# Keys in three tiles of 128 plus one shared rest tile, with the instruction order planned in passes

## The chip, the cores and the metric

The kernel runs on one core of one Trainium2 chip. The metric is device microseconds of that core for one execution. Runs of 3 to 5 rounds give an interval; executions of one kernel agree within about 0.3 to 0.5 %. "Faster" or "slower" needs more than 2 %. In the profiles PE is TensorE (the matmuls), ACT is ScalarE (exponentials, roots), DVE is VectorE and POOL is GpSimd (squares, sums, scalings), SP is SyncE (it issues transfers), and DMA stands for the transfers themselves.

## The reference

```python
def rmsnorm(x, g):
    return x / np.sqrt(np.mean(x * x, axis=-1, keepdims=True) + 1e-06) * g
q_n, k_n = rmsnorm(q, g_q), rmsnorm(k, g_k)         # q, k, v: 8 batches, 12 heads, 448 tokens, 64 dims, float32
scores = np.matmul(q_n, k_n.transpose(0, 1, 3, 2)) / 8
attn = softmax(scores)                              # written out in the reference
x = np.matmul(attn, v)                              # -> 3584 tokens x 768
h = x @ w_in                                        # 768 x 2048
out = (h * np.clip(h + 3.0, 0.0, 6.0) / 6.0) @ w_out    # 2048 x 768
```

A batch has six pairs of heads, so there are 48 pairs. The order of the keys does not matter as long as the values use the same order; both kernels use this freedom.

## The kernel before

Every instruction is a step given to a planner. The planner is a list scheduler: it walks forward in time, and on each engine it takes, of the steps that could start, the one with the smallest hand-set `due` time. The result is a fixed order per engine. On the chip each engine then runs its own list strictly in order and waits by semaphores.

```python
    NPE = 10
    GATE, W_IN_AT, W_OUT_AT, W_STEP = 2, 7.0, 35.0, 6.3
    START, FIRST, PAIR = 9.0, 4.1, 2.3
...
    def load_g():                                   # four small loads on ScalarE's queue
        for a in range(2):
            nc.scalar.dma_start(out=gq_t[a * 64:(a + 1) * 64, :], in_=g_q.rearrange("(p o) -> p o", o=1))
            nc.scalar.dma_start(out=gk_t[a * 64:(a + 1) * 64, :], in_=g_k.rearrange("(p o) -> p o", o=1))
...
    def heads(src, P):                              # keys: 4 tiles of 112; 1024 contiguous bytes per partition and head
        b, j = divmod(P, NJ)
        return src[b, 2 * j:2 * j + 2, :, :].rearrange("h (p t) d -> p h (t d)", t=T)
...
            def score(t0=t0, taken=taken):          # a cluster: four 64-row matmuls, two heads side by side
                for i, (ps, _, _) in enumerate(taken):
                    for a in range(2):
                        rows, c0 = slice(a * 64, a * 64 + 64), (t0 + i) * PT
                        nc.tensor.matmul(out=ps[:, a, 0:S], lhsT=kp[rows, c0:c0 + 128],
                                         rhs=kq[rows, 1, :], start=True, stop=True)
...
        def values(dst, c0, first):                 # 2 heads x 4 key tiles, for each of 4 query tiles: 32 matmuls
            for a in range(2):
                for t in range(T):
                    nc.tensor.matmul(
                        out=dst[:, a * E1:(a + 1) * E1], lhsT=e[0:PT, t, a, c0:c0 + 128], rhs=va[0:PT, a, t, :],
                        start=(first and a == 0 and t == 0), stop=(t == T - 1), skip_group_check=True)
...
    def weights(c, at, load, kept):                 # w_in and w_out, four loads of 768 KB each, on GpSimd's queue
        kept[c] = add("POOL", 0.9, at, lambda: load(c), gate, xfer=4.4, after=at)
```

The MLP of batch b is interleaved with the attention of batch b + 1. Batch 0's attention therefore runs alone. I call the time up to about 140 us the ramp; after that everything repeats every 50 us or so.

## Time and profile before

| stretch | PE busy | what runs |
|---|---|---|
| 0 to 11.7 us | 0.0 | loads, squares, root |
| 11.7 to 45.5 us | 26.2 of 33.8 | batch 0's attention alone |
| 45.5 to 80 us | 32.3 of 34.5 | first MLP, batch 1's attention |
| 80 to 376 us | 293.9 of 296 | steady state |
| 376 to 434 us | 57.9 of 58 | last MLP |

The median time is 441.08 us. The page of the kernel before, its parts 1 and 2: the busy time of TensorE, then 40 slices of 11 us each with the busy tenths of TensorE, the granted clock, the busy tenths of the DMA engines, and what they moved.

```profile
PE 410.6 (94%) x3663; PEld 229.2 (52%) x3682; DVE 246.3 (56%) x417; ACT 249.0 (57%) x425; POOL 240.2 (55%) x230
PE   0588799999999999999999999999999999999995
PEclk9999999999999999999999999999999999999999
DMA  8999999877545745674465655684465420220122
GB/s 241 247 265 261 224 214 193 216 197 192 128 121 148 189 113 136 167 214 111 133 156 157 177 135 145 159 214 109 120 161 164 97 56 12 54 81 0 37 72 73
```

TensorE is full from the sixth slice on. The DMA engines are full (tenths 8 and 9) from the first slice to the seventh, about 77 us.

The view by stretches of the same kernel (stretch, its length, busy us and instructions of PE, PEld, DVE, ACT, POOL, granted clock, DMA share, GB/s; the DMA share adds up the times of packets, which overlap, so it can exceed 1):

```profile
20.00:40.00 20.00, 18.30 (x250) 11.86 (x250) 17.98 (x36) 17.32 (x27) 17.83 (x18) 1.00 1.16 260
40.00:60.00 20.00, 15.79 (x186) 9.65 (x188) 17.52 (x30) 13.09 (x27) 19.45 (x22) 1.00 1.22 228
60.00:80.00 20.00, 19.84 (x207) 11.33 (x208) 14.55 (x27) 16.44 (x29) 16.86 (x16) 1.00 1.08 209
80.00:120.00 40.00, 39.46 (x353) 20.24 (x358) 27.10 (x39) 26.98 (x45) 27.46 (x24) 1.00 0.69 177
```

The timeline of GpSimd, reduced to the weight loads that it issues (start, length; the first, the last w_in, and the last w_out); each lands about 10 to 13 us later, the last at 69.3 us:

```profile
8.34 1.04 POOL L277 DMA_DIRECT2D w_in_sb<-in_moe_w_in_dram  x1
...
34.31 0.89 POOL L277 DMA_DIRECT2D w_in_sb<-in_moe_w_in_dram  x1
...
57.06 0.94 POOL L283 DMA_DIRECT2D w_out_sb<-in_moe_w_out_dram  x1
```

In the waits of 0 to 14 us (us in total, times, longest), ScalarE's first square waits 6.9 us behind its own g loads:

```profile
ACT sq L320 <- DMA gq_t<-in_g_q_dram: 6.9, 1, 6.9
```

In the groups by form (line, engine, operation, shapes, count, then busy us in total and mean ns of one), there are 192 exponentials, and VectorE's five squares of the ramp average 1354 ns:

```profile
L421 ACT ACTIVATE e<-S 112x896 bf16<-112x896 f32 x192 | 166.3, 914 | 64.1 <-PE S L416 64.0
...
L322 DVE TENSOR_TENSOR sq<-qk 112x512 f32<-112x512 f32 x5 | 6.8, 1354 | 0.0
```

### The profile page before, as it was taken

How to read it: one execution, taken by the hardware profiler on the slowest of the kernel's cores; microseconds unless marked ns; L12 is line 12 of the kernel's file. 1: busy time of each engine (PE TensorE's matmuls, PEld its weight loads, DVE VectorE, ACT ScalarE, POOL GpSimd, SP SyncE). 2: the span in 40 equal slices, each digit the busy share in tenths (PEclk: the TensorE clock that was granted, in tenths of full speed). 3: DMA queues.
4: the chain of work that ended last, by engine and by line, in shares of the span. 5: the costliest groups of instructions: out<-in, count | busy, mean ns of one | idle time of the engine just before them, and what ended most of it. 6: DMA issues, size and time to landing. Idle time of an engine off the chain costs nothing.

```text
span 438.6 us, 9205 instructions
## 1 busy us (share of the span) xinstructions
PE 410.6 (94%) x3663; PEld 229.2 (52%) x3682; DVE 246.3 (56%) x417; ACT 249.0 (57%) x425; POOL 240.2 (55%) x230
## 2 busy tenths in 40 slices
PE   0588799999999999999999999999999999999995
PEld 0355455555455565554455565554455555654563
DVE  1998887657674564456555465556564444334421
ACT  3788588657765666367664677357673665123200
POOL 3499988855757567656765657747757510000000
PEclk9999999999999999999999999999999999999999
DMA  8999999877545745674465655684465420220122
GB/s 241 247 265 261 224 214 193 216 197 192 128 121 148 189 113 136 167 214 111 133 156 157 177 135 145 159 214 109 120 161 164 97 56 12 54 81 0 37 72 73
DMA packets 102923, 64.58 MB, mean 147 GB/s; under 512 B 59744, under 2 KB 99424, under 8 KB 102880
## 3 DMA queue, kind: packets, MB, share of 16 engines
q1 hardware_dynamic: 94544, 57.01, 50.6%
q0 software_dynamic: 7296, 6.29, 9.1%
q10 hardware_dynamic: 1040, 0.69, 0.5%
q8 instruction: 29, 0.48, 0.5%
q14 instruction: 14, 0.11, 0.1%
HBM read 45.61 MB, written 11.01 MB: 129 GB/s over the span
## 4 chain that ended last, share of the span: by engine, by line
PE 80%; POOL 5%; DVE 4%; ACT 3%; issue 3%; DMA 3%; SPq 1%; POOLq 0%
PE M L558 27%; PE M L533 25%; PE S L416 9%; PE X L437 8%; PE S L558 4%; PE R L437 2%; PE S L533 2%; DVE ssq L337 1%; ACT e L421 1%; POOL qks L351 1%; PE X L558 1%; POOL sq L322 1%; POOL va L359 1%; DMA gq_t<-in_g_q_dram 1%; POOL sq L329 1%
## 5 line engine op out<-in xcount | busy, mean ns | idle before, releaser
L421 ACT ACTIVATE e<-S 112x896 bf16<-112x896 f32 x192 | 166.3, 914 | 64.1 <-PE S L416 64.0
L533 PE MATMUL M<-xT,w_in_sb 128*128 128x384 bf16 (+1 forms) x679 | 145.1, 349 | 3.7 <-DVE gT L541 2.9
L351 POOL TENSOR_TENSOR qks<-qk,rs 112x512 bf16<-112x512 f32 x87 | 90.5, 1055 | 86.6 <-ACT rs L344 84.7
L558 PE MATMUL M<-w_out_sb,gT 128*128 128x384 bf16 x736 | 131.8, 326 | 0.0
L558 PEld LDWEIGHTS <-gT 128*128 128x128 bf16 x896 | 82.9, 98 | 57.8 <-issue 7.8
L533 PEld LDWEIGHTS <-w_in_sb 128*128 128x128 bf16 x768 | 69.6, 97 | 67.4 <-issue 12.5
L541 DVE SCALAR_TENSOR_TENSOR gT<-t,M 128x384 bf16<-128x384 f32 (+1 forms) x116 | 70.6, 611 | 59.1 <-ACT t L539 58.3
L539 ACT ACTIVATE t<-M 128x384 f32<-128x384 f32 (+1 forms) x116 | 62.6, 540 | 67.0 <-PE M L533 65.5
L437 PEld LDWEIGHTS <-e 112*128 112x128 bf16 x1536 | 65.1, 99 | 31.4 <-issue 16.0
L337 DVE TENSOR_REDUCE ssq<-sq 112x16 f32<-112x1024 f32 (+1 forms) x49 | 58.4, 1193 | 23.3 <-POOL sq L329 12.2
L329 POOL TENSOR_TENSOR sq<-qk 112x1024 f32<-112x1024 f32 x36 | 68.1, 1892 | 0.0
L416 PE MATMUL S<-kq,kp 64*128 64x448 bf16 x384 | 56.6, 364 | 4.1 <-DVE kp L381 1.7
L437 PE MATMUL X<-va,e 112*128 112x65 bf16 x1152 | 58.6, 196 | 0.8 <-ACT e L421 0.6
L566 DVE COPY y<-M 128x384 f32<-128x384 f32 x46 | 25.6, 556 | 59.2 <-PE M L558 59.0
L359 POOL CAST va<-vf 112x512 bf16<-112x512 f32 x48 | 31.5, 658 | 10.4 <-DMA vf<-in_v_dram 10.1
L392 POOL TENSOR_SCALAR kp<-kq,gp 128x448 bf16<-128x448 bf16 x23 | 32.3, 1402 | 5.3 <-DMA kq<-qks 5.2
L463 DVE TENSOR_TENSOR xn<-X,rd 128x384 bf16<-128x384 f32 x48 | 26.8, 558 | 1.6
L416 PEld LDWEIGHTS <-kp 64*128 64x128 bf16 x384 | 12.2, 94 | 27.7 <-issue 18.0
L437 PE MATMUL R<-va,e 112*128 112x65 bf16 x384 | 20.4, 195 | 0.0
L377 PE MATMUL M<-ident,qks 112*128 112x112 bf16 x80 | 7.9, 242 | 13.0 <-DVE qks L351 12.4
L558 PE MATMUL S<-w_out_sb,gT 128*128 128x384 bf16 x112 | 19.5, 326 | 0.0
L462 DVE RECIPROCAL rd<-X 128x6 f32<-128x6 f32 x48 | 9.2, 192 | 15.3 <-PE X L437 15.2
(42 smaller groups left out, 156.2 us busy)
## 6 DMA issues: line engine op xcount, KB each, us to landing
qk<-in_k_dram SPq DMA_DIRECT2D x48, 224.0 KB, 3.3
vf<-in_v_dram SPq DMA_DIRECT2D x48, 224.0 KB, 3.7
qk<-in_q_dram SPq DMA_DIRECT2D x45, 224.0 KB, 3.4
w_in_sb<-in_moe_w_in_dram POOLq DMA_DIRECT2D x4, 768.0 KB, 11.3
w_out_sb<-in_moe_w_out_dram POOLq DMA_DIRECT2D x4, 768.0 KB, 11.9
out_dram<-y SPq DMA_DIRECT2D x8, 336.0 KB, 3.1
out_dram<-y SPq DMA_DIRECT2D x8, 288.0 KB, 3.4
out_dram<-y SPq DMA_DIRECT2D x8, 240.0 KB, 3.2
```

What stands on the lines that cost most here:

```text
L329: parts = [add("POOL", 1.93, at - 10, lambda: nc.gpsimd.tensor_tensor(out=sq[0:PT], in0=qk[0:PT], in1=qk[0:PT], op=MULT), *ld, *war, lock= ...
L337: red = add("DVE", 0.6 * n, at - 8 * hurry + 0.5 * i0, lambda i0=i0, i1=i1, cs=cs: nc.vector.tensor_reduce(out=ssq[0:PT, cs], in_=sq[0:PT, ...
L351: sc.append(add(on, 0, at - 6 * hurry, lambda e, i=i, rs4=rs4: engines[e].tensor_tensor(out=qks[0:PT, i].rearrange("p t h d -> p h t d"), ...
L359: vc = add({"POOL": 0.61}, 0, at - 3, lambda e: engines[e].tensor_copy(out=va[0:PT, :, :, 0:D], in_=vf[0:PT].rearrange("p h (t d) -> p h t ...
L392: nc.vector if e == "DVE" else nc.gpsimd).tensor_scalar_mul(
L416: nc.tensor.matmul(out=ps[:, a, 0:S], lhsT=kp[rows, c0:c0 + 128], rhs=kq[rows, 1, :], start=True, stop=True)
L421: x = add("ACT", 0.93, at + step * (t0 + i) / T + 0.2, lambda t=t0 + i, ps=ps: nc.scalar.activation(out=e[0:PT, t], in_=ps[0:PT, :, 0:S], ...
L437: nc.tensor.matmul(out=dst[:, a * E1:(a + 1) * E1], lhsT=e[0:PT, t, a, c0:c0 + 128], rhs=va[0:PT, a, t, :], start=(first and a == 0 and t ...
L533: nc.tensor.matmul(out=m[:, 0:n], lhsT=w_in_sb[:, kt, f * 128:(f + 1) * 128], rhs=X[:, kt, :], start=(kt == 0), stop=(kt == NKT - 1))
L539: r = add("ACT", 0.08 + n / 1200, due + span, lambda: nc.scalar.activation(out=t[:, 0:n], in_=m[:, 0:n], func=RELU, bias=0.5, scale=1.0 / ...
L541: g = add("DVE", 0.12 + n / 960, due + span, lambda: nc.vector.scalar_tensor_tensor(out=G[:, f, :], in0=t[:, 0:n], scalar=1.0, in1=m[:, 0: ...
L558: nc.tensor.matmul(out=m[:, 0:HALF], lhsT=G[:, f, i * 128:(i + 1) * 128], rhs=w_out_sb[:, f, cols], start=(f == 0), stop=(f == NFT - 1))
```

## The change

Intent: use all 128 rows of TensorE for the values, save a cluster of scores and an exponential per two pairs, start the squares earlier, and let the planner find its own due times. Keys 0 to 383 of a head become three full tiles; the remaining 64 keys of all twelve heads of a batch are loaded, normalized and transposed once per batch as one block-diagonal tile. A pair's rest scores are one 128-row matmul for both heads, and its rest values are eight half-height matmuls placed behind a score cluster.

```diff
-        return src[b, 2 * j:2 * j + 2, :, :].rearrange("h (p t) d -> p h (t d)", t=T)
+            in_=heads(src, P)[:, 0:SM].rearrange("h (p t) d -> p h (t d)", t=NS)), *war, xfer=(16, 768), after=after)]
+    def rest_loads(b):                       # once per batch, all heads: 256 contiguous bytes per partition and head
+            x = src[b, :, SM:S, :].rearrange("(j h) p d -> h p j d", h=2)
+            return [add("SP", 0.5, at, lambda a=a: nc.sync.dma_start(out=dst[a * 64:a * 64 + 64], in_=x[a]), *war,
+                        xfer=(24, 256), after=max(0.7, begin[b * NJ] - REST_AT)) for a in range(2)]
...
+    def order(self):                         # planning in passes: PASSES = 8
+        for n in range(self.PASSES):
+            got = self.forward()
+            ...                              # keep the pass with the earliest planned end
+            if n < self.PASSES - 1:
+                self.backward(got)           # rewrites every step's due: s.due = at - s.on[e], its latest start
...
-    GATE, W_IN_AT, W_OUT_AT, W_STEP = 2, 7.0, 35.0, 6.3
-    START, FIRST, PAIR = 9.0, 4.1, 2.3
+    GATE, W_IN_AT, W_OUT_AT, W_STEP = 4, 6.0, 40.0, 4.3
+    START, FIRST, PAIR = 9.0, 3.7, 2.1
...
-            nc.scalar.dma_start(out=gq_t[a * 64:(a + 1) * 64, :], in_=g_q.rearrange("(p o) -> p o", o=1))
+        return nc.gpsimd.dma_start(          # two loads, on GpSimd's queue
+            out=t[:], in_=g.rearrange("(a p o) -> a p o", a=1, o=1).to_broadcast([2, D, 1]))
...
+            if ins is not None and s.lock and s.eng in ("DVE", "POOL"):
+                if s.eng == "POOL" and holder is not None:      # GpSimd waits for VectorE's last two-input operation
+                    tc.add_manual_dep(ins.ins, holder.ins.name, ..., reason="port")
+                holder = ins if s.eng == "DVE" else None
```

(Cut: the rest tile's preparation, the sharing of seven exponentials by two pairs, a planner's model of the memory queues, new positions of several steps.)

## The prediction

> **What bounds the kernel now.** TensorE, except early. The page gives PE 410.6 of 438.6 us busy. The view by stretches splits the rest: 0 to 11.7 us PE idle; 11.7 to 45.5 us (batch 0's attention, no MLP to fill gaps) 26.2 of 33.8 busy; 45.5 to 80 us 32.3 of 34.5; 80 to 376 us 293.9 of 296; MLP tail to 434 us full; last copy and store 4.6 us. From start to start in the timeline, a value matmul (attention times values) holds PE 33 ns, a 384-column MLP matmul 162, a 512-column one 216, a cluster of four 64-row score matmuls 484, plus about 100 ns that the matmul before a cluster takes longer. The Trainium skill (TensorEngine Tiling, Key Properties) says that changing the tiling mode drains TensorE and that row tiles run in parallel; the trace agrees: four 448-column matmuls in 484 ns are two at a time.
>
> **Removed, added, moved, per pair of heads.** Before: 2 clusters (2 x 0.58) and 32 value matmuls (1.06): 2.2 us. After, by the instruction order: 3 clusters for two pairs (0.88 per pair), one full-height 448-column matmul for both heads' rest keys (0.19), 24 value matmuls (0.79), and 8 half-height ones directly behind a cluster, without a further mode switch (estimate 0.13 if they pair up, 0.26 if not). Sum 2.0 to 2.1: 0.1 to 0.23 saved, I take 0.18. 42 pairs run where PE is full: -7.5 us.
>
> ScalarE: 3.5 exponentials per pair instead of 4 (914 ns each), worth something only in batch 0, where ScalarE paces: 6 x 0.46 us, less 1 us for the rest's square and root: -1.5 us.
>
> Start: the waits table shows ScalarE's first square held to 8.89 us behind its own g-load issues, though k landed at 4.2 us. With g on GpSimd's queue the squares should start at 5.5 to 6 us, and the first exponential (14.9 us) at 11.5 to 12.5: -3 us, if batch 0's inputs keep up. DMA is over 90% busy to 80 us, but weight loads now come later.
>
> Gaps from 33 to 80 us come from GpSimd (90% busy) and VectorE colliding: VectorE's squares average 1.35 us against 0.68 undisturbed. Serializing and planning in passes: -1.5 us. GpSimd is 60% busy after 80 us, its work per pair about equal; its new waits should cost nothing there.
>
> **Prediction: 427.5 us, 8 times in 10 between 420 and 436; faster by over 2% 0.77, within 2% 0.20, slower 0.03.** Over half of the gain is steady state.
>
> **What would show it.** Start-to-start costs as above; 80 to 376 us still 99% PE. First exponential near 12 us, no g wait on ScalarE. 171 exponentials, not 192; ScalarE busy about 232 us, not 249. No VectorE square over 0.75 us; GpSimd waits named after VectorE, off the chain. MLP groups unchanged.
>
> **What would make it wrong.** The half-height value matmuls may not pair, or may drain twice: the steady gain halves. One exponential now serves both pairs' rest, and a pair's output bank is held from the rest's matmuls to the normalization: PE may stall on VectorE or ScalarE. More, smaller packets (768 and 256 B) may starve batch 0 or delay w_in and the first MLP group (45.5 us now). GpSimd waiting for VectorE may stretch the preparation of batches 1 and 2. The other way, if the new order removes nearly all early gaps, 420 is in reach.

## More of the kernel before

An MLP half is its w_in or its w_out matmuls.

## The result and the profile after

| | before | after |
|---|---|---|
| median of the same rounds, us | 440.89 (440.47 to 442.52) | 447.15 (446.58 to 448.34) |
| ratio of mean times, 95 % interval | | 1.0139 (1.0105 to 1.0172) |
| span of the profiled run, us | 438.6 | 446.3 |

The changed kernel is 1.4 % slower, which counts as "the same" at 2 %, and 11 us above the predicted range. A ratio here and below is the mean time of one kernel's fast runs over the mean of the other's fast runs of the same rounds, so it is not quite the ratio of the medians quoted.

The same parts of the page of the changed kernel:

```profile
PE 405.6 (91%) x3619; PEld 230.7 (52%) x3636; DVE 248.7 (56%) x469; ACT 233.5 (52%) x421; POOL 226.2 (51%) x286
PE   0597859879699999999999999999999999999996
PEclk9999998989999999999999999999999999999999
DMA  9969999999768778958945887679783311220122
GB/s 177 262 158 218 233 194 220 174 207 221 191 145 166 185 158 169 172 104 223 175 119 143 197 177 163 121 194 193 126 155 91 77 27 46 63 73 0 31 77 71
```

TensorE has 5 us less work and ScalarE 15.5 us less (predicted: 232 busy, measured 233.5). But TensorE now has holes up to the eleventh slice, and the clock drops twice. (The clock row says nothing of the start: its records begin only at 25.9 us before and 29.6 us after. Until then a 448-column score matmul lasts about 550 ns in both kernels, afterwards 360.) The DMA row has a dip in the third slice (22 to 33 us, 158 GB/s where it was 265) and is full to the tenth slice, about 110 us, instead of the seventh. The stretches say the same:

```profile
20.00:40.00 20.00, 17.25 (x236) 10.32 (x235) 17.44 (x38) 14.41 (x26) 13.60 (x19) 1.00 0.86 178
40.00:60.00 20.00, 15.79 (x191) 10.23 (x188) 19.21 (x38) 12.63 (x28) 14.33 (x19) 1.00 1.18 229
60.00:80.00 20.00, 15.41 (x153) 8.98 (x150) 11.21 (x23) 12.14 (x24) 11.42 (x13) 0.91 1.28 210
80.00:120.00 40.00, 32.50 (x288) 17.93 (x289) 16.48 (x31) 16.96 (x32) 28.00 (x34) 0.96 1.11 200
```

From 20 to 60 us TensorE lost about one us; from 60 to 120 us it lost 11.4 us (15.41 + 32.50 against 19.84 + 39.46).

**Where the time went.** The clearest way to see it is to take one event per batch, the last w_in matmul of that batch's MLP, in both traces, and subtract (after minus before, us):

| batch | 0 | 1 | 2 | 3 | 4 | 5 | 6 | last w_out matmul |
|---|---|---|---|---|---|---|---|---|
| after - before | +4.1 | +13.8 | +11.9 | +10.8 | +9.8 | +8.8 | +7.8 | +7.8 |

The whole loss of 13.8 us is made by the end of batch 1's first MLP half, at 140 us. From there on the changed kernel gains about 1 us per batch of six pairs, 6.0 us in all: 0.17 us per pair, where the prediction had 0.18. So the steady state is nearly as predicted, and the ramp is 14 us worse. Of these, 4.1 us are there at the end of batch 0's first MLP half, and 9.7 us join between batch 0 and batch 1, from 77 to 140 us. Keep the two parts apart: the experiments move them separately.

**The weight loads.** The first is issued 24 us later than before, all of them 11 to 24 us later, and the last lands at 93.9 us instead of 69.3 (the timeline of GpSimd again: the first and last w_in, the last w_out):

```profile
32.39 0.93 POOL L404 DMA_DIRECT2D w_in_sb<-in_moe_w_in_dram  x1
...
44.91 0.84 POOL L404 DMA_DIRECT2D w_in_sb<-in_moe_w_in_dram  x1
...
79.53 0.94 POOL L410 DMA_DIRECT2D w_out_sb<-in_moe_w_out_dram  x1
```

The hand-set earliest time of the first is 6 us; it is the backward pass that sets their due to the latest start its model allows. The plan has the last of them landing at 81 us; on the chip it lands 13 us later. By 60 us the DMA engines have moved 12.6 MB, before 14.7 MB (bytes of the packet records). From 60 to 140 us the engines then wait 29 us in all for loads and transposes, where it was under 3 us (waits of all engines added up).

**How a late landing stops TensorE.** The waits of 56 to 70 us of the changed kernel (who waited for whom, us in total, times, longest):

```profile
PE M L836 <- DVE gT L844: 5.2, 2, 4.2
...
POOL sqr L573 <- DMA kr<-in_k_dram: 4.2, 1, 4.2
...
DVE rsr L575 <- POOL sqr L573: 3.3, 1, 3.3
ACT rsr L579 <- DVE rsr L575: 2.6, 1, 2.6
```

Read it from the cause upwards. The two loads of batch 2's rest keys (`kr`) were issued at 51.3 and 52.0 us and landed at 60.4 and 62.7 us. GpSimd stood at their square (`sqr`), VectorE stood at the sum of that square, ScalarE at its root. Each runs its list in order, so the MLP's work that stood behind (ScalarE's `t`, VectorE's `gT`) waited too, though its inputs were there. The timeline of 62 to 67.5 us shows the end of the knot (start, length, idle before it and what ended that in brackets):

```profile
62.87 0.83 POOL L573 TENSOR_TENSOR sqr<-kr 128x384 f32<-128x384 f32 x1 [4.17 <-DMA kr<-in_k_dram]
63.73 0.55 DVE L575 TENSOR_REDUCE rsr<-sqr 128x6 f32<-128x384 f32 x1 [3.25 <-POOL sqr L573]
64.32 0.21 ACT L579 ACTIVATE rsr<-rsr 128x6 f32<-128x6 f32 x1 [2.61 <-DVE rsr L575]
64.67 0.47 ACT L842 ACTIVATE t<-M 128x384 f32<-128x384 f32 x1
66.52 1.01 DVE L844 SCALAR_TENSOR_TENSOR gT<-t,M 128x384 bf16<-128x384 f32 x2
67.11 0.80 PE L836 MATMUL M<-xT,w_in_sb 128*128 128x384 bf16 x2 [4.19 <-DVE gT L844]
```

Batch 2's rest is not needed by any matmul for another 20 us (even its transpose is issued only at 83.9 us). What hurts is its place in three in-order lists. After the gap the clock is low as well: matmuls that take 162 ns from start to start take about 320 ns for some 3.4 us, and the stretch has a granted clock of 0.91. The Trainium skill (TensorE: Matmul & The Clock Gate, Part 1) gives a window of about 3.4 us after which an idle TensorE falls to half its clock. Here the gap was 4.2 us, but a shorter one does it too: in fat_all below, a gap of 2.75 us (2.9 us from start to start) was followed by 3.4 us at half clock. So this gap of four us costs almost two more (an estimate: half of 3.4). The second drop of the clock follows a gap of 3.1 us that ends at 91.0 us: TensorE stood behind GpSimd's `kp`, whose transpose, issued at 79.2 us, took 10.4 us to land.

**What came out as predicted.** The exponentials are 171 (144 + 21 + 6) and no VectorE square is stretched:

```profile
L700 ACT ACTIVATE e<-S 128x896 bf16<-128x896 f32 x144 | 124.7, 915 | 36.7 <-PE S L667 36.7
...
L700 ACT ACTIVATE er<-S 128x896 bf16<-128x896 f32 x21 | 19.2, 915 | 10.2 <-PE S L672 9.8
...
L700 ACT ACTIVATE er<-S 128x448 bf16<-128x448 f32 x6 | 3.2, 541 | 0.6 <-PE S L672 0.4
...
L451 DVE TENSOR_TENSOR sq<-qf 112x512 f32<-112x512 f32 x4 | 2.8, 688 | 0.0
```

From start to start, 150 to 376 us, a pair's clusters, rest scores, full-height and half-height values take 0.63 + 0.19 + 0.82 + 0.24 = 1.88 us, against 1.00 + 1.13 = 2.13 us before. The half-height matmuls do run in pairs: 14 ns from start to start in the median, against 33 ns for a full-height one. The Trainium skill (TensorEngine Tiling (Array Packing), Key Properties) says that tiles run independently and that a change of tiling mode drains TensorE; with the transitions the eight of them average 29.5 ns. The saving of 0.25 us is more than the 0.17 us of the delays. Counted between the last w_in matmul of batch 2 and that of batch 6 (24 pairs), the attention took 5.5 us less, 0.23 per pair, but the w_in matmuls 1.7 us more, 0.75 of it a gap.

### The profile page after: what moved, and what is told of

Read it like the earlier page. It is cut to its first block, busy times and chain, and to the rows that moved or that the text cites. A ratio compares the mean times of both kernels' runs of the same rounds, so it can differ in the third digit from the quotient of the medians.

```text
span 446.3 us, 9321 instructions
## 1 busy us (share of the span) xinstructions
PE 405.6 (91%) x3619; PEld 230.7 (52%) x3636; DVE 248.7 (56%) x469; ACT 233.5 (52%) x421; POOL 226.2 (51%) x286
## 2 busy tenths in 40 slices
DMA packets 123340, 65.77 MB, mean 147 GB/s; under 512 B 77088, under 2 KB 119840, under 8 KB 123296
## 4 chain that ended last, share of the span: by engine, by line
PE 54%; DVE 4%; DMA 2%; SPq 2%; issue 1%; POOL 1%; ACT 0%; POOLq 0%; DVEq 0%
PE M L861 20%; PE M L836 15%; PE X L756 5%; PE S L861 4%; PE S L667 4%; PE S L836 2%; PE X L861 2%; DMA kq<-qks 1%; PE X L836 1%; DVE gT L844 1%; PE S L672 1%; DMA kr<-in_k_dram 1%; DVE ssq L467 1%; DVE xn L775 1%; PE X L639 1%
## 5 line engine op out<-in xcount | busy, mean ns | idle before, releaser
L700 ACT ACTIVATE e<-S 128x896 bf16<-128x896 f32 x144 | 124.7, 915 | 36.7 <-PE S L667 36.7
L467 DVE TENSOR_REDUCE ssq<-sq 128x14 f32<-128x896 f32 (+2 forms) x49 | 52.0, 1063 | 23.7 <-POOL sq L451 17.0
L756 PEld LDWEIGHTS <-e 128*128 128x128 bf16 x1152 | 48.9, 99 | 17.6 <-issue 5.3
L756 PE MATMUL X<-va,e 128*128 128x65 bf16 x1152 | 55.6, 196 | 0.0
L536 POOL TENSOR_SCALAR kp<-kq,gp 128x384 bf16<-128x384 bf16 x21 | 26.9, 1279 | 43.5 <-DMA kq<-qks 24.8
L488 POOL TENSOR_TENSOR qks<-qf,rs 112x512 bf16<-112x512 f32 x43 | 45.0, 1047 | 4.6 <-DVE sq L451 2.0
L503 POOL CAST va<-vf 128x384 bf16<-128x384 f32 x48 | 24.1, 508 | 44.3 <-PE X L756 41.7
L451 POOL TENSOR_TENSOR sq<-qf 112x512 f32<-112x512 f32 x41 | 43.1, 1051 | 4.0 <-issue 2.0
L481 POOL TENSOR_TENSOR qks<-kf,rs 128x384 bf16<-128x384 f32 x43 | 35.7, 831 | 13.3 <-ACT rs L474 11.9
L451 POOL TENSOR_TENSOR sq<-kf 128x384 f32<-128x384 f32 x41 | 33.9, 827 | 10.6 <-DVE ssq L467 6.6
L700 ACT ACTIVATE er<-S 128x896 bf16<-128x896 f32 (+1 forms) x27 | 22.5, 832 | 10.9 <-PE S L672 10.3
```

The costliest lines, as they stand in the source:

```text
L451: return engines[e].tensor_tensor(out=o, in0=x, in1=x, op=MULT)
L467: lambda i0=i0, i1=i1, rows=rows: nc.vector.tensor_reduce(out=ssq[0:rows, i0:i1], in_=sq[0:rows, i0:i1], axis=AX_X, op=ADD),
L481: return engines[e].tensor_tensor(out=qks[:, 0:NS].rearrange("p t (h d) -> p h t d", h=2), in0=kf[:].rearrange("p (h t) d -> p h t d", h=2 ...
L488: return engines[e].tensor_tensor(out=qks[0:PT, NS:QB].rearrange("p t (h d) -> p h t d", h=2), in0=qf[0:PT].rearrange("p (h t) d -> p h t ...
L700: lambda dst=dst, ps=ps, w=2 if whole else 1: nc.scalar.activation(out=dst, in_=ps[:, 0:w, 0:S], func=EXP), s, *(AVW[P] if t < NS else AVR ...
L756: nc.tensor.matmul(out=X[:, a, s * E1:(s + 1) * E1], lhsT=e[:, t, a, c0:c0 + 128], rhs=va[:, a * NS + t, :], start=False, stop=(t == NS - ...
```

## The experiments

Eighteen kernels ran. Except where it is said that a result is wrong, all were correct. The version w_early is called "early weights" below; many later ones build on it. Some of the quoted expectations name theories, and the letters change their meaning. In round 1, A is that the late weight loads are the cause, B that the added small packets are, C that GpSimd's new waits are. In round 2, A is that the backward passes are the cause, B that batch 2's rest loads block the engines. In round 3, C is that small packets are the cause, D its rival that only the plan's order counts. In round 4, E is that the planner counts on landings that come too early. A kernel that is planned anew gets another order on every engine, so it tests more than its edit; w_moved (but for the weight loads), no_port, before_port and the kernels with other packets keep the order.

### Round 1: what in the ramp costs

**w_moved: only the weight loads moved earlier in the finished plan.**

```diff
+        moved = [s for s in order if s in W_in.values() or s in W_out.values()]
+        for s, t in zip(moved, (10.3, 15.0, 21.5, 31.0, 36.0, 42.0, 48.0, 54.0)):
+            order.insert(next(i for i, x in enumerate(order) if x.start >= t and x not in moved), s)
```

> The changed kernel with the eight weight loads moved earlier in GpSimd's own instruction order (first one at about 11 us instead of 32.4), every other engine's order untouched. Theory A (the planner's backward passes made the weight loads as late as possible; between 20 and 33 us the DMA engines then have slack, and from 33 to 94 us the 6.3 MB collide with the next batches' loads and transposes; TensorE loses about 12 us there): 433 to 439 us, last weight load landed before 72 us, PE busy over 95% from 60 to 120 us. Rival B (the added small packets, 256 and 768 B, are too much DMA work whenever the weights come): under 3 us gained, so 444 to 447 us. Rival C (GpSimd's new waits for VectorE slow the preparation): under 3 us gained.

Measured: 447.12 us, ratio 1.0121 (1.0081 to 1.0161). A miss. The weights landed by 75.3 us and TensorE was busier from 80 to 120 us (37.3 of 40), but batch 1's loads had been planned for the queues without the weights: GpSimd waited 7.0 us for batch 1's rest keys, TensorE had a hole of 4.6 us at 31 us, and batch 0 ended 12.6 us late instead of 4.1, in part because the clock was at half for 6.8 us from 34.0 us on. In a saturated stretch, moving one load forward moves others back.

**w_early: the weights and their gate pinned to the times of the kernel before, everything else planned around them.**

```diff
-            s.due = at - s.on[e]
-            free[e] = s.due
+            begin = at - s.on[e]
+            if not s.pin:                    # pinned: the weight loads and their gate
+                s.due = begin
+            free[e] = begin
-    GATE, W_IN_AT, W_OUT_AT, W_STEP = 4, 6.0, 40.0, 4.3
+    GATE, W_IN_AT, W_OUT_AT, W_STEP = 2, 7.0, 35.0, 6.3
```

> The changed kernel planned anew with the weight loads pinned: the backward pass may not change their due time, they go out as soon as their earliest time of the kernel before is reached (7, 13.3, 19.6, 25.9, 35, 41.3, 47.6, 53.9 us), behind the gate of the kernel before. All engines' orders change with it. Theory A: 430 to 438 us. Rivals B and C: 443 us or more.

Measured: 442.19 us, ratio 1.0016 (0.9970 to 1.0063): 5 us better than the change, level with the kernel before, between what A and its rivals expected. Batch 1's delay fell from 13.8 to 6.5 us. The part that joins between batch 0 and batch 1 fell from 9.7 to 0.9 us; batch 0 itself got 1.6 us later. So the late weights are a part of the cause, and not all of it. The largest hole is again GpSimd at batch 2's rest keys (5.7 us wait; issued about 50 us, landed 64 and 66), so that hole is not the late weights' doing.

**before_late: the late weights put into the kernel before.**

```diff
-    GATE, W_IN_AT, W_OUT_AT, W_STEP = 2, 7.0, 35.0, 6.3
+    GATE, W_IN_AT, W_OUT_AT, W_STEP = 2, (31.5, 39.0, 43.0, 44.5), (51.0, 65.0, 70.5, 79.0), 0.0
```

> The kernel before with its weight loads issued no earlier than the changed kernel issued them (31.5, 39, 43, 44.5, 51, 65, 70.5, 79 us). Theory A: 8 to 14 us slower than before, 449 to 455 us, with PE idle between 57 and 120 us. Rival B (extra packets are needed for the loss): under 3 us slower. Rival C: no loss, since this kernel has no such waits.

Measured: 451.94 us, ratio 1.0231 (1.0186 to 1.0276): 10 us slower than the kernel before, though against 2 % the verdict is unclear. The delay is about 12.8 us from batch 2 to the end. Not all of it is the weights'. On the chip they were issued 4 to 9 us later than in the changed kernel, and the order was planned anew: the first score exponential came 1.6 us later (16.48 against 14.87 us), before any weight load, and batch 0's first MLP half ended 6.1 us late after this (timeline of 38 to 43 us, VectorE and TensorE):

```profile
38.36 3.59 DVE L351 TENSOR_TENSOR qks<-qk,rs 112x512 bf16<-112x512 f32 x2
...
42.57 0.56 PE L416 MATMUL S<-kq,kp 64*128 64x448 bf16 x2 [3.21 <-DVE kq L383]
```

Two scalings on VectorE took 3.59 us beside squares on GpSimd, where one alone takes about 0.9; TensorE stood, and the clock was at half for 10.2 us from 41.0 us on, with one weight load issued until then. What fits the weights is the 7.4 us that join between batch 0 and batch 1, against 9.7 us in the changed kernel. There the engines wait for late loads again (waits of 60 to 140 us; the kernel before waits there under 1 us for any load of q):

```profile
POOL sq L329 <- DMA qk<-in_q_dram: 8.0, 2, 5.1
```

**no_port: the change without GpSimd's waits for VectorE.**

```diff
-                if s.eng == "POOL" and holder is not None:
+                if False:
```

> The changed kernel, same order, without GpSimd's added waits for VectorE's two-input operations. Theory A: within 2 us of the changed kernel's 447 us, VectorE's squares stretched again. Rival C: 8 us or more faster.

Measured: 462.9 us, ratio 1.0456 (1.0390 to 1.0521), slower. A clear miss: in this order the waits are worth about 14 us (1.0456 less 1.0139, times 441). The timeline of VectorE from 33 to 40 us, and that of GpSimd after it, show why:

```profile
34.22 5.20 DVE L451 TENSOR_TENSOR sq<-qf 112x512 f32<-112x512 f32 x1
```

```profile
34.21 0.93 POOL L404 DMA_DIRECT2D w_in_sb<-in_moe_w_in_dram  x1
35.16 0.84 POOL L451 TENSOR_TENSOR sq<-kf 128x384 f32<-128x384 f32 x1
35.94 1.05 POOL L451 TENSOR_TENSOR sq<-qf 112x512 f32<-112x512 f32 x1
36.93 0.51 POOL L503 CAST va<-vf 128x384 bf16<-128x384 f32 x1
37.40 1.47 POOL L588 TENSOR_TENSOR krs<-kr,rsr 128x768 bf16<-128x768 f32 x1
```

A VectorE square that takes 688 ns alone took 5.20 us while GpSimd issued a weight load and ran four operations back to back. The loss of 14 us includes the clock, which was at half for 13.6 us in the ramp, against 6.8 us in the changed kernel. The Trainium skill (SBUF — State Buffer, "SBUF: two separate sides") calls the pair of ports that the two share an exclusive lock, held for a whole instruction. This run agrees that they hold each other up; that VectorE did not get its turn between GpSimd's operations is how I read the two timelines.

### Round 2: passes, rest loads, start

**passes1: the change planned in one forward pass.**

```diff
-    PASSES = 8
+    PASSES = 1
```

> The changed kernel planned in one forward pass (no backward passes, so nobody rewrites when a step is due; everything else of the change kept). Theory A (backward passes push weight loads and loads of the next batches to their latest start, so the memory side idles early and queues up at 50 to 90 us): faster than the changed kernel, 436 to 443 us, weight loads landed by 75 us. Rival (the passes remove gaps; the rest tile's loads and the waits are what costs): slower than the changed kernel, 448 to 456 us, with batch 0 or 1 late for lack of order.

Measured: 457.25 us, ratio 1.0337 (1.0283 to 1.0392). The theory that the passes as a whole are the culprit falls: without them the order is worse by 2 %. (It is no test of early weights: the w_in loads went out at 19 to 25 us, but the last w_out load landed only at 84 us.) The largest knot is in the waits of 68 to 90 us, and the clock was at half for 13.7 us from 76.2 us on:

```profile
POOL krs L588 <- DVE kp L536: 10.8, 1, 10.8
PE M L836 <- DVE gT L844: 10.8, 3, 10.3
DVE kp L536 <- DMA kq<-qks: 10.2, 1, 10.2
```

VectorE stood 10.2 us at a scaling (`kp`) whose DMA transpose had not landed, and the MLP's `gT` stood behind it. It is the same mechanism as in the changed kernel, with another load.

**rest_early30 and all_early: the rest loads of batches 2 and on sent earlier; then also g first.**

```diff
-    TURN, TURN2, REST_AT = (16, 2100), (16, 1000), 15
+    TURN, TURN2, REST_AT = (16, 2100), (16, 1000), 30
+            for s in res:                    # the rest loads
+                s.pin = b > 1
+                s.due -= 100.0 * s.pin
```

> The version with early weights (442.2 us), and for batches 2 and on the loads of the rest keys and values may go 30 us ahead of their batch instead of 15 and are not put off by the backward pass. Theory B (the loads of batch 2's rest, issued at about 50 us and landed at 64 to 66 us, block GpSimd, VectorE, ScalarE and then the MLP in order, a 3.6 us gap of TensorE): that gap goes, 435 to 439 us, faster than the kernel before by 0.4 to 1.4 %. Rival (the memory queues are simply full to 80 us, another load is late instead): within 2 us of 442.

> As the version with the early rest loads, and g's two loads are issued first on GpSimd's queue, ahead of its memsets, so that g should land at about 7 to 8 us instead of 10.5. Theory B with the start: the 3 to 4 us gap of TensorE at 8.5 to 12.5 us shrinks by 2 us and the end comes 0.5 to 2 us earlier than in the version with early rest loads, 433 to 438 us. Rival (batch 0 is paced by its loads of k, q and v, not by g): first exponential earlier but batch 0's end unchanged, no gain.

Measured: 443.73 us, ratio 1.0046 (1.0022 to 1.0070), and 443.02 us, ratio 1.0034 (0.9993 to 1.0075). Both miss; the rivals hold. Batch 2's rest landed at 55 us instead of 68 in rest_early30, and the hole behind it was gone, but VectorE then waited 4.3 us for a load of q (TensorE's hole: 4.2 us at 54 us), and batch 0's last v landed at 38 us instead of 31. The memory queues were full; a load that goes first makes another one last.

**before_port: GpSimd's waits put into the kernel before, nothing else.**

```diff
-        for s in plan.order():
-            s.fn(s.eng)
+        holder = None                        # the loop with the manual dependency, as in the change
```

> The kernel before with GpSimd made to wait for VectorE's preceding two-input operation, nothing else. Theory (in the kernel before GpSimd and VectorE overlapped but the plan kept most apart; VectorE squares average 1.35 us against 0.68): squares fall to 0.7 us, total within 2 us of 441. Rival (the waits themselves cost, stopping GpSimd in order): slower, 443 to 450 us.

Measured: 440.94 us, ratio 0.9975 (0.9953 to 0.9997). VectorE's squares fell from 1354 to 792 ns, and that was worth a quarter of a per cent, half of one at most. In the kernel before, VectorE's stretched squares were hardly on the critical path.

### Round 3: packets

The remaining suspect was the queues' throughput. In the packet records of the kernels before and after, a packet of 256, 768, 1024 and 3072 bytes takes 18, 36, 46 and 121 ns in the median, which is 14, 21, 22 and 25 bytes per ns. Most of the 256-byte packets are those of DMA transposes; the rest loads' own, before the first transpose of the changed kernel, take 19 ns in the median and 27 in the mean. The change turned the 1024-byte packets of k and v into 768-byte and 256-byte ones: 123340 packets in all, before 102923. In the first slice the engines are as busy as before (tenths 9 and 8) but move 177 instead of 241 GB/s. The Trainium skill (DMA: Bandwidth & Descriptors, "Why small descriptors are slow (HBM only)") puts a fixed overhead on each packet, 27 % at 256 bytes by its arithmetic. The four sizes here agree in direction.

The four kernels below change nothing but which bytes a load fetches: same sizes, same number of loads, same order of instructions. All four give a wrong result.

**before_512 and before_2048: the kernel before with half-size packets for k and v, and with double-size ones for q, k and v.**

```diff
+        h0 = min(2 * j, 8)                   # before_512, k and v: 4 heads x 2 tokens instead of 2 heads x 4 tokens
+        return src[b, h0:h0 + 4, 0:S // 2, :].rearrange("h (p t) d -> p h (t d)", t=2)
-        return src[b, 2 * j:2 * j + 2, :, :].rearrange("h (p t) d -> p h (t d)", t=T)
+        return src[b, 2 * j:2 * j + 2, :, :].rearrange("h s d -> (h s) d").rearrange("(p n) d -> p (n d)", n=2 * T)
```

> The kernel before with its k and v loads fetching 512-byte pieces instead of 1024-byte ones: same bytes, same number of loads, same order of instructions (wrong result on purpose: the pieces are of other heads). Theory C (in the ramp the memory queues are the limit, and smaller packets move fewer bytes in the same busy time; 256, 768 and 1024 bytes took 18, 36 and 46 ns in the traces): 443 to 450 us, packets +21504, bytes moved by 60 us below the 14.7 MB of the kernel before, and TensorE gaps between 45 and 120 us. Rival D (packets are not the limit; the plan's order of the loads is): within 1.5 us of the kernel before.

> The kernel before with k, q and v loads in 2048-byte pieces (wrong result on purpose: both heads' rows mixed), same bytes, loads and order. Theory C: DMA's busy time falls by 5 to 10 us over the span and the ramp can only win: 437 to 441 us. Rival D: within 1.5 us.

Measured: 443.66 us, ratio 1.0024 (0.9996 to 1.0053), and 442.38 us, ratio 1.0003 (0.9970 to 1.0036). Both are what the rival said. The bytes by 60 us did move as the packet theory has it (14.35 and 14.95 MB against 14.70), but TensorE from 60 us on was as full as ever. The kernel before has slack in its landings.

**rest_fat and fat_all: early weights, with the rest loads in 1536-byte packets, then the main k and v loads too.**

```diff
-            x = src[b, :, SM:S, :].rearrange("(j h) p d -> h p j d", h=2)
+            x = src[b, 0:2, 0:SM, :].rearrange("a (p n) d -> a p (n d)", n=NJ)
-            in_=heads(src, P)[:, 0:SM].rearrange("h (p t) d -> p h (t d)", t=NS)), *war
+            in_=heads(src, P).rearrange("h s d -> (h s) d")[0:2 * SM].rearrange("(p n) d -> p (n d)", n=2 * NS)), *war
```

> The version with early weights (442.2 us), with the rest loads of keys and values fetching 1536-byte pieces instead of 256-byte ones: same bytes, loads and order (wrong result on purpose). Theory C: 2 to 4 us faster, 438 to 441 us. Rival D: within 1.5 us of 442.

> As before, and the k and v loads of three tiles in 1536-byte pieces instead of 768 as well (wrong result on purpose), same bytes, loads and order. Theory C: 4 to 8 us faster than the version with early weights, 434 to 438 us, bytes moved by 60 us near the 14.7 MB of the kernel before, and batch 0's MLP ending near 73 to 75 us instead of 78.5. Rival D: within 2 us of 442.

Measured: 440.17 us, ratio 0.9945 (0.9913 to 0.9978), and 436.36 us, ratio 0.9863 (0.9834 to 0.9892), against 1.0016 for early weights. Both times hit: 3 us and 7 us, though early weights were measured in another set of rounds. By 60 us 14.7 MB were moved, as expected, but batch 0's first MLP half ended at 77.0 us and not at 73 to 75. The stretches of fat_all beside those of early weights (w_early first):

```profile
60.00:80.00 20.00, 15.96 (x166) 9.13 (x166) 12.36 (x27) 11.37 (x23) 10.58 (x15) 0.91 1.13 220
80.00:120.00 40.00, 38.01 (x360) 21.18 (x360) 22.96 (x46) 23.00 (x42) 33.20 (x40) 1.00 0.90 193
```

```profile
60.00:80.00 20.00, 16.96 (x179) 10.02 (x177) 13.35 (x29) 12.78 (x25) 12.13 (x16) 0.91 1.21 222
80.00:120.00 40.00, 40.00 (x388) 22.09 (x387) 25.54 (x48) 25.83 (x46) 33.98 (x42) 1.00 0.84 191
```

TensorE is now completely full from 80 to 120 us. This is not a usable kernel, but it shows that the same structure and the same order, fed in larger pieces, beats the kernel before by 1.4 %. One hole of 2.75 us remains at 69.8 us, where VectorE and GpSimd again wait for a transpose.

### Round 4: do the causes add up, and can the order be mended?

**after_fat: the large packets in the change as it stands, with its late weights** (the edit of fat_all, without early weights; wrong).

> The changed kernel as it stands (weights late) with 1536-byte pieces for the main and the rest loads (wrong result on purpose), same bytes, loads and order. If packets and late weights add up: 6 to 8 us faster than the changed kernel, 438 to 442 us. If the late weights alone set the ramp here, the packets hardly matter: 445 to 447 us.

Measured: 448.32 us, ratio 1.0113 (1.0074 to 1.0151), against 1.0139 for the change. The intervals overlap: the large packets gain about 1 us here, and the intervals allow up to 3, where they gained 7 us behind early weights. The causes do not add up. As long as the weights are late, they set most of the ramp; only once they are early does the rate of the other loads show in full.

**g_first: early weights, g's loads issued before GpSimd's memsets.**

```diff
+    for s in g_load:                         # due -16, issued at 0.7 and 1.7 us
+        s.pin = True
```

> The version with early weights (442.2 us) with g's two loads issued first on GpSimd's queue. If g's late landing (10.5 us, a TensorE gap of 3 to 4.5 us before 12.5 us) costs at the end: 439 to 441 us. If batch 0 is paced by its own loads afterwards: within 1.5 us of 442.

Measured: 444.57 us, ratio 1.0048 (1.0018 to 1.0078). TensorE's first hole shrank, but the newly planned order brought batch 0's v at 42 us instead of 31, and batch 0's first MLP half ended 9.6 us late instead of 5.6, with the clock at half for 10.2 us from 40.5 us on. The earlier start did not pay; whether it would in an unchanged order is not shown.

**rest_late_g, cal110_g, cal110, cal115: the planner told that loads land later.**

```diff
-                        xfer=(24, 256), after=...
+                        xfer=(24, 256), late=5.0 if b in (1, 2) else 0.0, after=...        # rest_late_g, with g first
-        cost = size * 4e-5 if s.eng == "POOL" and size > 64 else 0.034 + size * 1.56e-5
+        cost = 1.1 * (size * 4e-5 if s.eng == "POOL" and size > 64 else 0.034 + size * 1.56e-5)    # cal110; 1.15: cal115
```

> As g_first, and the planner is told that the rest loads of batches 1 and 2 land 5 us later than its model says, so that it puts their users behind other work; nothing is issued earlier. Theory E (in-order engines blocked by a landing planned too early): the 3.6 us gap near 65 us goes, 435 to 440 us, and this beats the kernel before. Rival (the bytes are late whatever the order): within 1.5 us of g_first.

> As g_first, with every memory time of the planner's model raised by 10 %. Theory E: the ramp's landings match the plan better, 435 to 440 us. Rival (the bytes are late whatever the order; a slower model only reorders the ramp at random): 440 to 445 us.

> The version with early weights (442.2 us, ratio 1.0016) with every memory time of the planner's model raised by 10 %, nothing else. Theory E (the plan counts on landings that come later than it thinks): 0.990 to 0.997 of the kernel before. Chance: 1.000 to 1.006.

> The same with 15 %. Theory E: again 0.990 to 0.998, as the lateness of the landings is of that size. Chance: anything from 0.995 to 1.010, unrelated to the 10 % version.

Measured, with g first: rest_late_g 443.42 us, ratio 1.0024 (0.9994 to 1.0053); cal110_g 441.53 us, ratio 0.9976 (0.9947 to 1.0005). Without: cal110 444.04 us, ratio 1.0043 (1.0008 to 1.0078); cal115 444.66 us, ratio 1.0062 (1.0039 to 1.0086). The first pair looked like a way to mend the order; the second pair, the same edit alone, is no better than early weights without it (1.0016). The theory that a slower model of the landings cures the order finds no support. What these edits do is to draw another order, and the orders tried differ by about 0.4 % either way. cal110_g is not shown to beat anything.

The delay of the last w_in matmul of a batch, against the kernel before, for the versions that the argument rests on (us, from the profiled runs):

| version | batch 0 | batch 1 | batch 2 | batch 6 | from batch 1 to the last w_out |
|---|---|---|---|---|---|
| after | +4.1 | +13.8 | +11.9 | +7.8 | -6.0 |
| w_moved | +12.6 | +12.1 | +10.0 | +5.7 | -6.4 |
| w_early | +5.6 | +6.5 | +4.9 | +0.2 | -6.3 |
| fat_all | +4.0 | +2.6 | +0.9 | -3.2 | -5.7 |
| after_fat | +5.2 | +11.6 | +9.5 | +5.1 | -6.5 |
| no_port | +13.6 | +23.3 | +21.4 | +17.5 | -5.7 |
| passes1 | +17.8 | +18.3 | +16.6 | +16.3 | -1.9 |
| g_first | +9.6 | +10.3 | +8.9 | +4.3 | -5.9 |
| before_late | +6.1 | +13.5 | +12.8 | +12.7 | -0.7 |

The last column is the steady state: the gain is there in every kernel with the new tiles, 5.7 to 6.5 us in this table (3.9 to 6.7 us in the seven that are not in it), except passes1, which gains less. In the kernel before with late weights it is not. The first columns are the ramp, and they hold most of the differences between versions. Batch 0 is at least 4.0 us late in every version with the new tiles, early weights and large packets or not. What changes with the weights is the step from batch 0 to batch 1: +9.7 us in the changed kernel, +7.4 in before_late, +0.9 in w_early, -1.4 in fat_all.

## Why the prediction was wrong, point by point

**Steady state, -7.5 us: right in mechanism and nearly in size.** It gave 6.0 us from batch 1's first MLP half to the end. Per pair 0.17 us against 0.18; that these are so close is partly luck, as the attention saved 0.23 us and the w_in matmuls took a part back. The half-height matmuls pair up, as the trace shows directly.

**ScalarE, -1.5 us: the counts were right (171, 233.5 us busy), the gain is not seen.** Batch 0's attention ended at 42.8 us against 43.1.

**Start, -3 us: the first exponential came 1.25 us earlier** (13.62 against 14.87) **and by the end of batch 0's attention 0.3 us were left.** The first square did start at 4.4 us. But g, put on GpSimd's queue, landed at 9.1 and 10.6 us, and VectorE waited 2.8 us for it. Sending g first did not pay either (g_first), so the step "the first exponential at 11.5 to 12.5" failed first at g and then at "if batch 0's inputs keep up".

**Gaps from 33 to 80 us, -1.5 us: this is the step that failed.** The prediction put these gaps down to GpSimd and VectorE colliding. before_port shows that removing that collision from the kernel before is worth 0.25 %. In the changed kernel the gaps come instead from landings: an engine stands in order at an operation whose load or transpose is late, and the MLP's operations behind it wait. The prediction took 6 us off the ramp in all (3 for the start, 1.5 for ScalarE, 1.5 for these gaps); instead it grew by 13.8 us.

**"DMA is over 90% busy to 80 us, but weight loads now come later": seen, and read the wrong way round.** The prediction took the later weights as relief for batch 0. With the DMA engines saturated, bytes not moved at 20 to 40 us (178 against 260 GB/s) have to be moved at 60 to 110 us, when the MLP, the next batch and the transposes want them. before_late loses 7.4 us in the stretch where this acts, w_early gets 5 of the lost 6 us back, and all eight orders planned with early weights end at 1.0062 or below, against 1.0139. The prediction never checked how long the queues stay full when 6.3 MB of weights start 24 us later.

**"More, smaller packets may starve batch 0 or delay w_in and the first MLP group": named as a risk, and real, but second in line.** With early weights the packets are worth 7 us (fat_all), with late ones about 1 us (after_fat), and in the kernel before about 1 us (before_512, with an interval from 0 to 2).

**The waits: "its new waits should cost nothing there" was right** (after the ramp the gain is 6.0 us with them and 5.7 without), and they were worth more than thought: without them this order loses another 14 us (no_port).

**What stays open.** Late weights and, behind them, small packets make up most of the ramp's loss, and no correct version tried is clearly faster than the kernel before; the best are before_port (0.9975) and cal110_g (0.9976, interval reaching 1). The 4 us at batch 0 that stay in fat_all go with a late transpose (a hole of 2.75 us, then 3.4 us at half clock); no run removes them. Whether some order of the new structure with its 768- and 256-byte packets reaches fat_all's 436 us is open: eight planned orders with early weights (w_early and its seven variants with unchanged packets) ended between 0.9976 and 1.0062. Why the kernel before tolerates smaller packets and the new one does not is argued, not shown: its lists leave more time between landing and use, and it has no once-per-batch load.

## What to carry to other kernels

A saving on the bottleneck engine in steady state is only half of an estimate; add up the bytes that the ramp needs and ask what a new order does to them, because a load put off in a saturated ramp is paid back later with interest. When engines run fixed lists in order, a planner that pushes loads to their latest start turns every late landing into a stop for whatever stands behind it, even work whose inputs are there. Judge ramp and steady state apart, by the delay of one event per batch: it told in one table that the tiles were good and the start was not.

## What the Trainium skill lacked or had wrong

- SBUF — State Buffer, "SBUF: two separate sides": it tells of the exclusive lock, but gives no size for what happens when GpSimd runs back to back. Here a VectorE square of 688 ns took 5.20 us beside a weight load's issue and four GpSimd operations in a row, and the order that made GpSimd wait was 14 us faster.
- DMA: Bandwidth & Descriptors gives the overhead of a small packet by arithmetic for 256 bytes; medians in these traces are 18, 36, 46 and 121 ns for 256, 768, 1024 and 3072 bytes (at 256 bytes mostly transposes). It gives no figure for a load that stands behind others in full queues: from issue to landing a rest load of 96 KB took 3.8 us in the median of the changed kernel, and 14 us in w_early between 50 and 66 us, where the queues were full.
- DMA: Bandwidth & Descriptors, "Issuing engines are not separate DMA queues" fits the traces (rest loads on SyncE's queue took 9 to 14 us when issued at 51 to 53 us in the changed kernel, with weights of GpSimd's queue in flight, and under 4 us at 19 to 21 us, with none), but no page gives a size for this: the DMA transposes issued in the changed kernel from 79 to 84 us, while the last weights were in flight, took 10 to 12 us, where the medians of their kinds are 2.7 to 4.3 us.
- TensorE: Matmul & The Clock Gate gives an idle window of about 3.4 us; in these traces less was enough: holes of 2.75 us (fat_all) and 4.2 us (the changed kernel) were both followed by 3.4 us at half clock, in which matmuls of 162 ns took about 320 ns. In before_late the half clock began 1.6 us after a hole began and lasted 10.2 us.
